# Stores of two chunks with eight tokens per partition, in a scan and mixture-of-adapters kernel

## The chip, the cores and the metric

The kernel runs on one core of a Trainium2 chip. A core has a matrix engine (TensorE, PE in the profile, with its weight loads as PEld), VectorE (DVE), ScalarE (ACT), GpSimd (POOL), and SyncE (SP), which here only issues DMAs. 16 DMA engines move data between HBM and the on-chip memory SBUF; TensorE writes to PSUM, from which VectorE and ScalarE read. The metric is the device time of one execution in microseconds (us), lower is better, given as the median of several runs.

## The reference

Two layers one after the other, on 8 sequences of 6400 tokens with 128 features, all f32:

```python
h = 0                                   # per sequence, 128 features
for t in range(S):
    h = a[:, t] * h + b[:, t]
    x[:, t] = h
# x as (51200, 128)
logits = x @ w_gate                     # 8 experts
topk = the 2 largest of each token;  w = softmax over those two
delta = sum over the 2:  w * ((x @ A[e]) @ B[e])      # A[e]: 128 x 16, B[e]: 16 x 128
out = x + delta
```

The first part is a linear recurrence along the tokens; the second sends each token through two of eight small rank-16 adapters. Inputs a and b are 26.2 MB each and the output is 26.2 MB, so 78.6 MB cross between HBM and the core.

## The kernel before

The 51200 tokens are cut into 100 chunks of 512 tokens (C), and a chunk into four blocks of 128 tokens (J = 4). A chunk is loaded so that partition p holds tokens 4p to 4p + 3 of it, 2 KB in a row; block j then is token 4p + j of every partition p. Most loads take two chunks of a or of b (512 KB), into six buffers each (a_tm, b_tm).

For each chunk (function front):

- A and B: TensorE transposes the four blocks of a and of b against the f32 identity into PSUM (pA, and pB with two buffers), so that features lie on partitions and the 512 tokens of the chunk in order along the row.
- ae: ScalarE copies pA to SBUF (a_st).
- sc: VectorE runs the recurrence over the 512 tokens with one scan instruction (line 442) and writes x in f16 to a ring of 24 chunk buffers (xT). The first value is the last column of the chunk before, so scans form one chain through the whole run. Every 6400 tokens a sequence begins anew; where that falls inside a chunk, its scan is split.

The rest works on units of six blocks (at the end of four), and on groups of four units, 24 blocks or six chunks (at the end of two and one):

- Z (zlogits, line 462): for each block one matmul, with the block of x as the weights that are loaded into TensorE and the adapters A with the gate (128 x 136) as the moving operand. This gives x A for all eight experts and the logits, tokens on partitions. Since tokens of a block are every fourth column of xT, the weight load reads every fourth f16.
- ze: ScalarE copies the result to SBUF (zl).
- gating (g1 to g4 and g6 on VectorE, w1 and w2 on ScalarE, g5, p1, p2, p3 on GpSimd): the largest and second largest logit of each token, the two weights, and a table g of 8 weights per token.
- mu (line 533): GpSimd multiplies zl with g, into zw (f16).
- T (line 543): TensorE transposes the six blocks of zw into pT; te copies them to zwT, on VectorE for three units of a group and on ScalarE for one.
- D (line 558 and 559): for each block, a matmul with the block of x as weights against the f16 identity, which brings x back to tokens on partitions, and on top of it a matmul of zwT with the adapters B. The sum is the output.
- oe (line 569): ScalarE copies it to outt, a ring of 72 blocks.
- st (line 595): SP issues the store of two chunks (of one for the last four).

The order of the work is written out by a planner, a list scheduler inside the kernel file (class Program). Every operation is added with its engine, an assumed duration, what it depends on, and a due time: the start of its period of six chunks (PERIOD) plus an offset from a table (TEMPLATE). For each engine the planner takes the operation that can start first among those whose due time lies within a window (WINDOW) of the earliest one left. LOAD_RATE and STORE_RATE are the DMA rates that it assumes. The result is a fixed order for each engine; semaphore waits are worked out from it. SP issues all loads and stores but the first of b in one queue, so a store that waits holds back the loads behind it.

At the start TensorE runs 34 transposes of the identity (line 359) before and between its first operations.

Of the kernel before, what the change touches and what calls it, by code (L numbers as in the profile page):

```python
# [7 lines left out]
F32 = mybir.dt.float32  # L8
F16 = mybir.dt.float16

PERIOD = 6
# [3 lines left out]
PE_WAIT = 0.08  # L15
SCAN_SELF = 0.13
ISSUE = {"sp": 0.52, "act": 0.45}
LOAD_RATE = 386e3
STORE_RATE = 420e3
DMA_START = 0.3  # L20
DMA_SEEN = 1.15
DMA_DEPTH = 9
FIRST_ISSUE = 0.7
WINDOW = {'pe': 22.339, 'act': 15.032, 'dve': 17.853, 'pool': 31.507, 'sp': 21.093}
START = (-999, "", 0)
FIRST = -9999
TAPER = [2, 2, 1, 1, 1, 1]
# [3 lines left out]
WARM0 = 12  # L31
WARM = 34
LAST = 2
TEMPLATE = {
    "la": [-13.768, -11.488, -10.699],
    "lb": [-11.599, -10.876, -10.408],
    "A": [-8.739, -5.735, -4.61, -4.527, -4.01, -3.388],
    "B": [-0.753, -0.06, 2.522, 2.886, 3.39, 4.151],
    "ae": [6.378, 8.693, 8.757, 9.146, 10.126, 12.233],
    "sc": [11.891, 15.28, 15.373, 17.047, 17.106, 17.222],  # L40
    "Z": [8.614, 8.864, 13.261, 13.471],
    "ze": [17.232, 19.133, 19.801, 20.09],
    "g1": [13.208],
    "g2": [18.458],
    "g3": [3.74],
    "g4": [5.014],
    "g5": [35.276],
    "g6": [5.048],
    "w1": [11.688],
    "w2": [17.689],  # L50
    "p1": [18.712],
    "p2": [4.238],
    "p3": [33.725],
    "mu": [17.377, 18.243, 18.627, 23.065],
    "T": [19.784, 21.14, 23.513, 25.169],
    "te": [11.814, 12.075, 12.746, 13.615],
    "D": [22.711, 24.793, 26.772, 27.207],
    "oe": [23.268, 23.347, 25.158, 27.374],
    "st": [18.431, 19.751, 20.387],
    "ta": [11.3, 11.673, 14.3, 15.8],  # L60
    "md": [10.222, 11.5, 13.0, 14.5],
    "wu": [-0.392],
    "ch": [5.145],
}


# [143 lines left out]
def bass_associative_scan_2x2__then__mixture_of_adapters_kernel(  # L210
# [8 lines left out]
    NB, S, D = a.shape  # L219
# [3 lines left out]
    T = NB * S  # L223
    C = 512
# [11 lines left out]
    b0 = 0  # L236
# [4 lines left out]
    NU = len(units)  # L241

    GMAX = 4
    groups = []
    u0 = 0
    for n in [GMAX] * ((NU - sum(TAPER)) // GMAX) + TAPER:
# [9 lines left out]
    NL = 6  # L256
    HC = 2
    NA = 3
    NX = 24
    NZ = 120  # L260
    NG = 5
    NW = 3
# [10 lines left out]
    with ExitStack() as stack:  # L273
# [19 lines left out]
        a_tm = sbuf("a_tm", [128, HC, J, D], F32, NL)  # L293
        b_tm = sbuf("b_tm", [128, HC, J, D], F32, NL)
        a_st = sbuf("a_st", [128, C], F32, NA)
        xT = sbuf("xT", [128, C], F16, NX)
        zl = sbuf("zl", [128, NZ, W], F32)
        zw = sbuf("zw", [128, U, 128], F16, NW)
        zwT = sbuf("zwT", [128, U * 128], F16, NW)
# [72 lines left out]
        def get(d, k):  # L372
            return [(d[k], True)] if k in d else []

        def xblock(b):
            return xT[b // J % NX].rearrange("d (p j) -> d j p", j=J)[:, b % J, :]

        def te_act(u):
            return u // GMAX < (NU - sum(TAPER)) // GMAX and u % GMAX in TE_ACT
# [31 lines left out]
        def front(c):  # L411
            sl = c // HC % NL
            r0 = rows[c]

            def trans(dst, src):
                def f():
                    dv = dst.rearrange("d (p j) -> d j p", j=J)
                    for j in range(J):
                        last = eng["pe"].transpose(dv[:, j, :], src[:, j, :], ident_f[:, :])  # L419
# [12 lines left out]
            x = xT[c % NX]  # L432
            starts = sorted({0} | {n * S - r0 for n in range(NB) if 0 < n * S - r0 < C})
            segs = list(zip(starts, starts[1:] + [C]))

            def scan():
                for s0, s1 in segs:
                    if (r0 + s0) % S == 0:
                        init = 0.0
                    else:  # L440
                        init = xT[(c - 1) % NX][:, C - 1 : C]
                    last = eng["dve"].tensor_tensor_scan(  # L442
                        out=x[:, s0:s1], data0=a_st[c % NA][:, s0:s1], data1=pB[c % 2][:, s0:s1],
                        initial=init, op0=ALU.mult, op1=ALU.add,
                    )
                return last

            o_sc[c] = P.add("dve", f"sc{c}", 1.276 + 0.16 * (len(segs) - 1),
                            [(o_ae[c], True), (o_B[c], True)] + get(o_sc, c - 1)
                            + get(xlast, c % NX),  # L450
                            scan, fr(c, "sc"))
# [70 lines left out]
        def back(gi, u):  # L522
# [38 lines left out]

            o_D[u] = P.add("pe", f"D{u}", 0.112 * n, [(o_te[u], True)] + get(o_oe, u - 1), delta, ba(gi, u, "D"))
            for k in range(n):
                xlast[(b0 + k) // J % NX] = o_D[u]
            o0 = b0 % NO

            def oe():
# [13 lines left out]
            while True:  # L581
                c = stored[0]
                m = 2 if c < NCH - 4 else 1
                if c >= NCH or (c + m) * J > b0 + n:
                    break
                store(c, m)
                stored[0] += m

        def store(c, m):
            q = c * J % NO  # L590
# [2 lines left out]
            op = P.add(  # L593
                "sp", f"st{c}", m * C * D * 4 / STORE_RATE, [(x, True) for x in src.values()],
                lambda: eng["sp"].dma_start(
                    out[r0 : r0 + m * C, :].rearrange("(h p j) d -> p h j d", p=128, j=J),
                    outt[:, q : q + m * J, :].rearrange("p (h j) d -> p h j d", j=J)),
                (PERIOD * (c // PERIOD), "st", c % PERIOD // 2), sem=dma_sem(f"st{q // (2 * J)}" if m == 2 else f"stx{c % 4}"),
            )
            o_st[c] = op  # L600
            for k in range(m * J):
# [3 lines left out]
        for gi, (u0, n) in enumerate(groups):  # L605
            for u in range(u0, u0 + n):
                b0, m = units[u]
                while nf * J < b0 + m:
                    if nf < 4:
                        load(nf, 1)  # L610
                    elif nf >= NCH - LAST:
# [7 lines left out]
            gating(gi)  # L619
            for u in range(u0, u0 + n):  # L620
                back(gi, u)

        P.schedule()
        waits = P.waits(s_eng, s_dma)
# [64 lines left out]
```

## Time and profile before

| | |
|---|---|
| median of 3 runs | 208.33 us (208.28 to 208.99) |
| profiled execution | 209.08 us |
| its span, first to last instruction | 206.9 us |
| granted TensorE clock, mean | 0.992 |
| busy PE, DVE, ACT, POOL | 94%, 87%, 83%, 64% of the span |
| HBM read and written | 52.56 and 26.21 MB, 381 GB/s over the span |
| pair store, issue to landing (median) | 11.2 us |
| single store, issue to landing (median) | 2.6 us |
| scan of 512 tokens | 1275 ns |

How to read it: the page shows the span in 40 slices, 5.2 us each, with the busy share of each engine in tenths, and the bytes moved by DMA in each slice. A group line names the source line, the engine, the operation, what it writes and reads, its shape and count, then busy time and mean duration, then the idle time of the engine before such instructions and what ended it. Matmuls are pipelined: one is recorded for some 220 to 280 ns, but the next starts 56 to 109 ns after it, so the time that TensorE needs is counted by starts. "Idle before" matters only on an engine that sets the pace.

### The profile page before, as it was taken

To read this page: it belongs to the slowest core of one execution; us is meant where nothing else is said; L and a number is where in the kernel's file an instruction comes from. 1 tells how busy PE (TensorE), PEld (TensorE's weight loads), DVE (VectorE), ACT (ScalarE), POOL (GpSimd) and SP (SyncE) were. 2 spreads that over 40 slices of the span, in tenths; PEclk is the share of its full clock that TensorE was granted. 3 is DMA by queue.
4 is the path that set the end of the run, shared out by engine and by line. 5 is a ranking of instruction groups with operands and counts; after the bars stand their busy time and mean duration, and the time that the engine had idled before them with its cause. 6 is when DMAs were issued, how large, how long until landed. Compare 5 with 4: busy or idle time off the path is not lost.

```text
span 206.9 us, 6064 instructions
## 1 busy us (share of the span) xinstructions
PE 194.1 (94%) x2434; PEld 185.8 (90%) x2434; DVE 179.2 (87%) x266; ACT 172.5 (83%) x295; POOL 132.8 (64%) x156
## 2 busy tenths in 40 slices
PE   6988699999999999999999999999999999998762
PEld 6976589999999999999999999999999999997641
DVE  0379959999999999999999999999998989978871
ACT  2266949979999999999989898989998989898552
POOL 1000194868686776859594949494959494879960
PEclk9999969999999999999999999999999999999999
DMA  6999999999999999999999999999999999999784
GB/s 195 376 388 385 388 387 387 386 395 399 397 397 400 405 394 403 395 402 403 395 407 398 405 395 404 402 400 406 398 405 400 405 401 401 406 406 389 303 333 159
DMA packets 42251, 79.17 MB, mean 383 GB/s; under 512 B 3696, under 2 KB 3824, under 8 KB 42224
## 3 DMA queue, kind: packets, MB, share of 16 engines
q1 hardware_dynamic: 40752, 78.39, 100.0%
q10 hardware_dynamic: 1472, 0.40, 0.8%
q8 instruction: 19, 0.31, 0.6%
q14 instruction: 8, 0.07, 0.1%
HBM read 52.56 MB, written 26.21 MB: 381 GB/s over the span
## 4 chain that ended last, share of the span: by engine, by line
PE 88%; ACT 4%; DVE 3%; POOL 2%; issue 2%; DVEq 0%; POOLq 0%
PE pB L419 21%; PE pA L419 21%; PE pZ L462 12%; PE pO L558 11%; PE pT L543 10%; PE pO L559 10%; PE pO L359 3%; DVE xT L442 2%; POOL zw L533 1%; ACT zl L468 1%; ACT outt L569 1%; ACT a_st L430 1%; DVE zwT L552 1%; ACT L506 1%; POOL g L518 0%
## 5 line engine op out<-in xcount | busy, mean ns | idle before, releaser
L442 DVE TENSOR_TENSOR_SCAN xT<-a_st,xT,pB 128x512 f16<-128x512 f32 x96 | 120.3, 1253 | 9.1 <-PE pB L419 3.5
L533 POOL TENSOR_TENSOR zw<-zl,g 128x768 f16<-128x768 f32 (+1 forms) x66 | 96.3, 1488 | 1.6
L430 ACT COPY a_st<-pA 128x512 f32<-128x512 f32 x100 | 60.5, 605 | 16.2 <-PE pA L419 14.6
L419 PE MATMUL pA<-ident_f,a_tm 128*128 128x128 f32 x400 | 61.7, 277 | 1.7 <-ACT a_st L430 1.5
L569 ACT COPY outt<-pO 128x768 f32<-128x768 f32 (+1 forms) x68 | 55.0, 808 | 9.3 <-PE pO L559 7.7
L419 PE MATMUL pB<-ident_f,b_tm 128*128 128x128 f32 x400 | 61.3, 279 | 1.2 <-DVE xT L442 1.1
L468 ACT COPY zl<-pZ 128x816 f32<-128x816 f32 (+1 forms) x68 | 57.9, 851 | 2.7 <-PE pZ L462 2.4
L558 PE MATMUL pO<-ident_h,xT 128*128 128x128 f16 x400 | 52.2, 220 | 3.6 <-ACT outt L569 1.5
L559 PE MATMUL pO<-cst_h,zwT 128*128 128x128 f16 x400 | 52.0, 219 | 0.0
L558 PEld LDWEIGHTS pO<-ident_h,xT 128*128 128x128 f16 x400 | 44.5, 113 | 5.4 <-ACT outt L569 2.7
L419 PEld LDWEIGHTS pA<-ident_f,a_tm 128*128 128x128 f32 x400 | 45.3, 143 | 3.8 <-issue 2.2
L419 PEld LDWEIGHTS pB<-ident_f,b_tm 128*128 128x128 f32 x400 | 44.3, 143 | 2.7 <-DVE xT L442 1.5
L501 POOL TENSOR_TENSOR dd<-m 128x24 f32<-128x24 f32 (+2 forms) x21 | 7.0, 333 | 51.2 <-DVE m L499 51.2
L559 PEld LDWEIGHTS pO<-cst_h,zwT 128*128 128x128 f16 x400 | 39.3, 98 | 0.0
L462 PE MATMUL pZ<-cst_h,xT 128*128 128x136 f16 x400 | 35.2, 224 | 0.8 <-DVE xT L442 0.4
L543 PE MATMUL pT<-ident_h,zw 128*128 128x128 f16 x400 | 33.5, 219 | 1.0 <-POOL zw L533 0.9
L552 DVE COPY zwT<-pT 128x768 f16<-128x768 f16 (+1 forms) x53 | 28.1, 530 | 5.0 <-PE pT L543 4.8
L462 PEld LDWEIGHTS pZ<-cst_h,xT 128*128 128x128 f16 x400 | 29.7, 114 | 1.9 <-DVE xT L442 0.9
L543 PEld LDWEIGHTS pT<-ident_h,zw 128*128 128x128 f16 x400 | 26.3, 98 | 2.5 <-POOL zw L533 1.8
L514 POOL TENSOR_TENSOR t<-k,w 128x192 f32<-128x192 f32 (+2 forms) x21 | 9.5, 453 | 11.6 <-ACT w L506 11.2
L442 DVE TENSOR_TENSOR_SCAN xT<-a_st,pB 128x512 f16<-128x512 f32 (+1 forms) x8 | 7.5, 939 | 5.6 <-ACT a_st L430 5.5
L549 ACT COPY zwT<-pT 128x768 f16<-128x768 f16 x15 | 12.2, 815 | 0.0
(22 smaller groups left out, 80.9 us busy)
## 6 DMA issues: line engine op xcount, KB each, us to landing
a_tm<-in_a_dram SPq DMA_DIRECT2D x48, 512.0 KB, 11.2
b_tm<-in_b_dram SPq DMA_DIRECT2D x48, 512.0 KB, 11.2
out_dram<-outt SPq DMA_DIRECT2D x48, 512.0 KB, 11.2
a_tm<-in_a_dram SPq DMA_DIRECT2D x4, 256.0 KB, 4.5
out_dram<-outt SPq DMA_DIRECT2D x4, 256.0 KB, 2.6
b_tm<-in_b_dram SPq DMA_DIRECT2D x3, 256.0 KB, 5.5
b_tm<-in_b_dram ACTq DMA_DIRECT2D x1, 256.0 KB, 3.6
cst_f<-in_moe_A_dram ACTq DMA_DIRECT2D x1, 64.0 KB, 4.5
```

The source lines that it names most:

```text
L419: last = eng["pe"].transpose(dv[:, j, :], src[:, j, :], ident_f[:, :])
L430: lambda: eng["act"].copy(a_st[c % NA][:, :], pA[:, :]), fr(c, "ae"))
L442: last = eng["dve"].tensor_tensor_scan(out=x[:, s0:s1], data0=a_st[c % NA][:, s0:s1], data1=pB[c % 2][:, s0:s1], initial=init, op0=ALU.mul ...
L462: last = eng["pe"].matmul(pZ[:, k // (n // 2), o : o + W], xblock(b0 + k), Awg_h)
L468: return eng["act"].copy(zl[:, zb : zb + n, :].rearrange("p (h k) w -> p h (k w)", h=2), pZ[:, :, 0 : n // 2 * W])
L533: lambda: eng["pool"].tensor_tensor(out=wv, in0=zv, in1=gv, op=ALU.mult), ba(gi, u, "mu"))
L543: last = eng["pe"].transpose(pT[:, k * 128 : k * 128 + 128], zw[w][:, k, :], ident_h[:, :])
L549: lambda: eng["act"].copy(zwT[w][:, 0 : n * 128], pT[:, 0 : n * 128]), ba(gi, u, "ta"))
L552: lambda: eng["dve"].tensor_copy(zwT[w][:, 0 : n * 128], pT[:, 0 : n * 128]), ba(gi, u, "te"))
L558: eng["pe"].matmul(dst, xblock(b0 + k), ident_h[:, :], start=True, stop=False)
L559: last = eng["pe"].matmul(dst, zwT[w][:, k * 128 : k * 128 + 128], B_h, start=False, stop=True)
L569: return eng["act"].copy(outt[:, o0 : o0 + n, :].rearrange("p (h k) w -> p h (k w)", h=2), pO[:, :, 0 : n // 2 * 128])
```

## The change

Chunks are joined into pairs (SUP = 2), except the last four, which stay single (SUP_TAIL). A buffer of x now holds a pair, 1024 tokens, and there are 12 of them instead of 24 of one chunk. A block of a pair takes every eighth token: block k is token 8p + k of the pair for every partition p. Loads, transposes and scans stay as they were, chunk by chunk; a scan writes its half of the pair's buffer. Since a block now has tokens of both chunks, Z of a unit depends on the scan of the last chunk of the pair that its last block belongs to (ready). The weight loads of x in Z and D read every eighth f16 of a row. In the output ring a partition holds the eight tokens 8p to 8p + 7 in a row, so a pair store writes 4 KB from each partition to 4 KB of HBM, where it wrote two rows of 2 KB.

The planner's tables (TEMPLATE, WINDOW, LOAD_RATE, STORE_RATE) have other values, so the order of the work changes on every engine. After the last D, TensorE issues 40 transposes of the f32 identity or parts of it (probe): 12 of 64 rows, 4 of 128, 12 of 32, 6 of 128 and 6 of 64. Nothing reads what they write.

```diff
-LOAD_RATE = 386e3
-STORE_RATE = 420e3
+LOAD_RATE = 392e3
+STORE_RATE = 410e3
-WINDOW = {'pe': 22.339, 'act': 15.032, 'dve': 17.853, 'pool': 31.507, 'sp': 21.093}
+WINDOW = {'pe': 39.992, 'act': 58.192, 'dve': 31.37, 'pool': 40.466, 'sp': 30.329}
+SUP = 2
+SUP_TAIL = [1, 1, 1, 1]
 TEMPLATE = {
...
+    supers = []
+    c0 = 0
+    for n in [SUP] * ((NCH - sum(SUP_TAIL)) // SUP) + SUP_TAIL:
+        supers.append((c0, n))
+        c0 += n
+    of_chunk = {c0 + k: i for i, (c0, n) in enumerate(supers) for k in range(n)}
+    ready = {b: supers[of_chunk[b // J]][0] + supers[of_chunk[b // J]][1] - 1 for b in range(NBLK)}
...
-    NX = 24
+    NX = 12
...
-        xT = sbuf("xT", [128, C], F16, NX)
+        xT = sbuf("xT", [128, SUP * C], F16, NX)
...
+        def xcols(c):
+            i = of_chunk[c]
+            o = (c - supers[i][0]) * C
+            return xT[i % NX][:, o : o + C]
+
         def xblock(b):
-            return xT[b // J % NX].rearrange("d (p j) -> d j p", j=J)[:, b % J, :]
+            i = of_chunk[b // J]
+            c0, n = supers[i]
+            return xT[i % NX][:, 0 : n * C].rearrange("d (p j) -> d j p", j=n * J)[:, b - c0 * J, :]
...
         def zlogits(u):
             b0, n = units[u]
-            c1 = (b0 + n - 1) // J
+            c1 = ready[b0 + n - 1]
...
-                    out[r0 : r0 + m * C, :].rearrange("(h p j) d -> p h j d", p=128, j=J),
-                    outt[:, q : q + m * J, :].rearrange("p (h j) d -> p h j d", j=J)),
+                    out[r0 : r0 + m * C, :].rearrange("(p j) d -> p j d", p=128),
+                    outt[:, q : q + m * J, :]),
...
+        def probe(pos):
+            def f():
+                for k in range(12):
+                    h = k % 2
+                    eng["pe"].transpose(
+                        pB[h][:, 0:64], ident_f[64 * h : 64 * h + 64, :], ident_f[64 * h : 64 * h + 64, 64 * h : 64 * h + 64])
+                for k in range(4):
+                    eng["pe"].transpose(pA[:, 0:128], ident_f[:, :], ident_f[:, :])
+                for k in range(12):
+                    h = k % 4
+                    dst = (pB[0], pB[1], pA, pT[:, 0:1024].bitcast(F32))[h]
+                    eng["pe"].transpose(
+                        dst[:, 0:32], ident_f[32 * h : 32 * h + 32, :], ident_f[32 * h : 32 * h + 32, 32 * h : 32 * h + 32])
+                for k in range(6):
+                    eng["pe"].transpose(pA[:, 0:128], ident_f[:, :], ident_f[:, :])
+                for k in range(6):
+                    last = eng["pe"].transpose(pB[0][:, 0:64], ident_f[0:64, :], ident_f[0:64, 0:64])
+                return last
+            return f
+
+        P.add("pe", "mb", 3.0, [(o_D[uN], True), (o_sc[NCH - 1], True), (o_te[uN], True), (o_ae[NCH - 1], True)],
+              probe(0), (9999, "", 0))
```

More of the change, by code (lines that the diff above doesn't have):

```diff
@@ L33 @@
 LAST = 2
+SUP = 2
+SUP_TAIL = [1, 1, 1, 1]
 TEMPLATE = {
[L35 to L63, printed above, removed]
+    "la": [-10.95, -9.437, -8.191],
+    "lb": [-10.023, -9.436, -7.903],
+    "A": [-11.026, -8.648, -7.41, -6.832, -6.44, -5.405],
+    "B": [-14.825, -14.817, -14.221, -14.015, -13.001, -10.71],
+    "ae": [-7.284, -6.693, -6.603, -5.642, -5.031, -4.184],
+    "sc": [13.472, 14.407, 15.428, 17.663, 19.382, 19.457],
+    "Z": [18.437, 19.004, 20.556, 22.524],
+    "ze": [51.529, 54.024, 54.601, 57.134],
+    "g1": [25.622],
+    "g2": [7.661],
+    "g3": [5.296],
+    "g4": [1.145],
+    "g5": [43.458],
+    "g6": [25.384],
+    "w1": [16.708],
+    "w2": [54.97],
+    "p1": [39.689],
+    "p2": [7.051],
+    "p3": [12.642],
+    "mu": [18.896, 19.36, 19.457, 24.196],
+    "T": [28.309, 28.632, 31.127, 33.058],
+    "te": [24.866, 24.891, 26.352, 29.891],
+    "D": [31.247, 32.555, 33.577, 36.679],
+    "oe": [46.479, 48.831, 48.877, 50.195],
+    "st": [21.173, 26.136, 27.083],
+    "ta": [11.3, 12.233, 14.3, 15.8],
+    "md": [9.107, 11.5, 13.0, 14.5],
+    "wu": [19.523],
+    "ch": [-28.476],
+    "mb": [0.0],
 }
@@ L243, in bass_associative_scan_2x2__then__mixture_of_adapters_kernel @@
     GMAX = 4
+    supers = []
[3 more added lines that the diff above has]
+        c0 += n
+    assert c0 == NCH
+    of_chunk = {c0 + k: i for i, (c0, n) in enumerate(supers) for k in range(n)}
+    ready = {b: supers[of_chunk[b // J]][0] + supers[of_chunk[b // J]][1] - 1 for b in range(NBLK)}
     groups = []
@@ L430, in front @@
                             lambda: eng["act"].copy(a_st[c % NA][:, :], pA[:, :]), fr(c, "ae"))
-            x = xT[c % NX]
+            x = xcols(c)
             starts = sorted({0} | {n * S - r0 for n in range(NB) if 0 < n * S - r0 < C})
@@ L440, in scan @@
                     else:
-                        init = xT[(c - 1) % NX][:, C - 1 : C]
+                        init = xcols(c - 1)[:, C - 1 : C]
                     last = eng["dve"].tensor_tensor_scan(
@@ L449, in front @@
                             [(o_ae[c], True), (o_B[c], True)] + get(o_sc, c - 1)
-                            + get(xlast, c % NX),
+                            + get(xlast, of_chunk[c] % NX),
                             scan, fr(c, "sc"))
@@ L563, in back @@
             for k in range(n):
-                xlast[(b0 + k) // J % NX] = o_D[u]
+                xlast[of_chunk[(b0 + k) // J] % NX] = o_D[u]
             o0 = b0 % NO
@@ L580, in back @@
                 olast[(b0 + k) % NO] = o_oe[u]
[L581 to L587, printed above, removed]
+            while stored[0] < len(supers) and sum(supers[stored[0]]) * J <= b0 + n:
+                store(*supers[stored[0]])
+                stored[0] += 1
         def store(c, m):
@@ L595, in store @@
                 lambda: eng["sp"].dma_start(
-                    out[r0 : r0 + m * C, :].rearrange("(h p j) d -> p h j d", p=128, j=J),
-                    outt[:, q : q + m * J, :].rearrange("p (h j) d -> p h j d", j=J)),
-                (PERIOD * (c // PERIOD), "st", c % PERIOD // 2), sem=dma_sem(f"st{q // (2 * J)}" if m == 2 else f"stx{c % 4}"),
+                    out[r0 : r0 + m * C, :].rearrange("(p j) d -> p j d", p=128),
+                    outt[:, q : q + m * J, :]),
+                (PERIOD * (c // PERIOD), "st", c % PERIOD // 2), sem=dma_sem(f"st{q // (SUP * J)}" if m == SUP else f"stx{c % 4}"),
             )
@@ L607, in bass_associative_scan_2x2__then__mixture_of_adapters_kernel @@
                 b0, m = units[u]
-                while nf * J < b0 + m:
+                while nf <= ready[b0 + m - 1]:
                     if nf < 4:
@@ L621, in bass_associative_scan_2x2__then__mixture_of_adapters_kernel @@
                 back(gi, u)
+        def probe(pos):
[17 more added lines that the diff above has]
+            return f
+        uN = NU - 1
+        P.add("pe", "mb", 3.0, [(o_D[uN], True), (o_sc[NCH - 1], True), (o_te[uN], True), (o_ae[NCH - 1], True)],
+              probe(0), (9999, "", 0))
         P.schedule()
```

## The prediction

> **What bounds the kernel now.** I read the page's slices first, then the three matmul weight-load groups, then the busy time of each engine by stage, then VectorE's and TensorE's timelines. The slices say that three resources are full at once:
>
> ```profile
> span 206.9 us, 6064 instructions
> ...
> PE   6988699999999999999999999999999999998762
> ...
> DVE  0379959999999999999999999999998989978871
> ...
> DMA  6999999999999999999999999999999999999784
> GB/s 195 376 388 385 388 387 387 386 395 399 397 397 400 405 394 403 395 402 403 395 407 398 405 395 404 402 400 406 398 405 400 405 401 401 406 406 389 303 333 159
> ```
>
> The DMA engines are busy from about 2 us to about 187 us: 387 GB/s while only loads run, some 401 GB/s once stores (a third of the bytes) are mixed in. The stages:
>
> ```profile
> 96.00:132.00 36.00, 35.99 (x481) 35.79 (x480) 34.53 (x49) 33.86 (x57) 25.65 (x26) 1.00 1.05 401
> ...
> 156.00:186.00 30.00, 29.61 (x388) 28.46 (x386) 27.05 (x45) 27.23 (x47) 22.03 (x23) 1.00 1.05 403
> 186.00:206.90 20.90, 13.40 (x178) 10.67 (x176) 13.39 (x35) 11.66 (x27) 13.47 (x28) 1.00 0.79 298
> ```
>
> (columns: stretch, length, busy PE, PEld, DVE, ACT, POOL, clock, DMA share, GB/s). A busy PE overlaps its own instructions, so I use the spacing of matmul starts: 109 ns for an f32 transpose, 56 for an f16 matmul, 59 for the 136-wide one. Six chunks hold 48, 72 and 24 of these: 10.7 us. VectorE takes the same time for six chunks, without a gap:
>
> ```profile
> 100.16 1.27 DVE L442 TENSOR_TENSOR_SCAN xT<-a_st,xT,pB 128x512 f16<-128x512 f32 x1
> 101.35 0.53 DVE L552 COPY zwT<-pT 128x768 f16<-128x768 f16 x1
> 101.80 1.27 DVE L442 TENSOR_TENSOR_SCAN xT<-a_st,xT,pB 128x512 f16<-128x512 f32 x1
> 103.00 0.56 DVE L552 COPY zwT<-pT 128x768 f16<-128x768 f16 x1
> 103.47 2.69 DVE L442 TENSOR_TENSOR_SCAN xT<-a_st,xT,pB 128x512 f16<-128x512 f32 x2
> 106.08 0.53 DVE L552 COPY zwT<-pT 128x768 f16<-128x768 f16 x1
> ...
> 109.12 0.33 DVE L489 TENSOR_REDUCE m<-zl 128x24 f32<-128x192 f32 x1
> 109.49 0.36 DVE L491 TENSOR_TENSOR k<-zl,m 128x192 f32<-128x192 f32 x1
> ...
> 110.94 1.27 DVE L442 TENSOR_TENSOR_SCAN xT<-a_st,xT,pB 128x512 f16<-128x512 f32 x1
> ```
>
> From 100.16 to 110.94 is one period of six chunks, 10.78 us, or 1.80 us a chunk. DMA needs 786 KB a chunk: 1.96 us at 401 GB/s. So the compute engines lead at 1.80 from chunk 48 to 72 (91.3 to 134.4 us, living on loads made ahead), and DMA leads after that: the A transposes of chunks 72 and 99 start at 134.4 and 186.5, 1.93 us a chunk. From 186 us a dependent tail of small groups ends the run, with every engine under 65% busy.
>
> **The change, part by part.**
>
> *Store packets.* 48 pair stores go from 256 packets of 2 KB to 128 of 4 KB. The trace's packet records have medians of 27 ns for 512 B and 84 for 2,048; the least of the 8,192 B instruction fetches took 309. The line through these gives 159 to 160 ns for 4,096 B, against 2 x 84 = 168: 8.5 ns saved per pair of packets, 128 x 8.5 / 16 engines = 0.07 us a store, 3.3 us for all 48. Bounds: nothing (packets overlap: the DMA share is 1.05), or 309/2 = 154.5 ns, 5.2 us in all. I take 3.3, as the 2 KB and 8 KB rows lie on both sides.
>
> The Trainium skill ("DMA: Bandwidth & Descriptors", Why small descriptors are slow) states a fixed overhead of about 3 cycles a packet. At the 850 MHz of that page (Where 436 GB/s comes from) this is an estimated 3.5 ns, 1.3 us in all; the intercept of the trace's rows is 8 ns. By the page the forecast would be about 1.3 us higher.
>
> *Order of the DMAs.* In SP's built order 34 pair stores stood before the last load and 14 behind it; now it is 32 and 16. Two stores fewer are 2 x 0.524 MB at 401 GB/s, 2.6 us. With 32 x 0.07 = 2.2 us, DMA lets the last load land 4.8 us earlier. (A store waits for both its chunks in either kernel; SP's queue holds behind it only loads, as before.)
>
> *May compute follow?* At 1.80 us instead of 1.93, chunks 72 to 99 take 3.5 us less. By the built order TensorE has, when it starts chunk 99's A, done 342 blocks of T and 330 of D instead of 354 and 348: 12 x 0.056 + 18 x 0.112 = 2.7 us less. Together 6.2; DMA's 4.8 is the smaller, so the front ends 4.8 us earlier.
>
> *VectorE's order.* Gating steps now alternate with scans (in letters, S scan, t zwT copy, digits gating: S t S S 1 t S S 2 3 S 4 t 6, before S t S t S S t S S 1 2 3 4 6). Pitches from the timeline: scan then scan 1.41, scan then something else 1.20, copy then scan 0.45, a gating step before its dependent 0.37 to 0.39, before something else 0.27. The new period sums to 10.4 instead of 10.78 us. What is late next is TensorE at 10.7: worth at most 0.1 us a period, no more.
>
> *Weight loads of x.* A block of x was read every fourth f16 (8 bytes apart), now every eighth (16 bytes). No row has a 16-byte step. The nearest:
>
> ```profile
> L558 PEld LDWEIGHTS pO<-ident_h,xT 128*128 128x128 f16 x400 | 44.5, 113 | 5.4 <-ACT outt L569 2.7
> L419 PEld LDWEIGHTS pB<-ident_f,b_tm 128*128 128x128 f32 x400 | 44.3, 143 | 2.7 <-DVE xT L442 1.5
> L543 PEld LDWEIGHTS pT<-ident_h,zw 128*128 128x128 f16 x400 | 26.3, 98 | 2.5 <-POOL zw L533 1.8
> ```
>
> Packed f16 98 ns, 8-byte step 113, f32 143. What counts is how long the load alone holds back its matmul. A matmul after idle shows it:
>
> ```profile
> 201.65 0.25 PE L558 MATMUL pO<-ident_h,xT 128*128 128x128 f16 x1 [0.52 <-DVE zwT L552]
> 201.73 0.22 PE L559 MATMUL pO<-cst_h,zwT 128*128 128x128 f16 x1
> ```
>
> It is recorded from its load's start to its end: 250 ns against 220 in a run, so 30 ns of load; by the same subtraction in the trace's records packed f16 has 15 and f32 331 - 273 = 58. In a run a load starts 2 ns after the matmul ahead started, so it is hidden while it is below the slot, 56 ns (59 for Z). Below: 30 ns again, cost 0. Above: the 109 ns spacing of the f32 transposes, if loads rather than matmuls set it: 400 x 53 + 400 x 50 = 41 us. I take 58 (f32's row, and about twice 30, as 30 is twice 15): 2 to 4 ns over the slot in D, none to 1 in Z, 24 x 4 ns = 0.1 us a period. TensorE goes from 10.7 to 10.8, which VectorE took before: 0 in the sum. Its cover is that 0.1 us; beyond, each ns on all 800 loads is 0.8 us on the path.
>
> The Trainium skill ("SBUF — State Buffer", Specifications) wants at least two hits in a 16-byte line for full bandwidth: that speaks against a 16-byte step, which has one. Its Door 1 section lists a stride of 8 bf16 as free in the same breath. No row here decides it. By the first reading the sum loses what lies over the slot, by the second nothing.
>
> *The ring of x* holds 12 pairs instead of 24 chunks and frees them by pair. D of the first block starts at 32.4 us, the scan that reuses its place is that of chunk 24, whose A starts at 47.4: 15 us cover a delay of one chunk, cost 0; without the cover, one chunk, 1.8 us.
>
> *Start.* Pairs delay Z: before the first T, TensorE now issues 60 B and 48 Z blocks instead of 56 and 42, 4 x 0.109 + 6 x 0.059 = 0.8 us. Ends: 0 (it waits there anyway, 18.65 busy of 22 us from 8 to 30), and one scan pitch, 1.4. I take 0.4.
>
> *Tail.* What was deferred returns: after the last B the order has 61 T, 70 D, 16 Z, 4 A blocks instead of 46, 52, 12, 0: 3.5 us of TensorE; VectorE gets three more copies and four small gating steps after the last scan, about 2.6 us. Ends: 0 (engines are under 65% busy) and 3.5. I take 3.0, for the tail is a dependent chain.
>
> *The 40 transposes of the identity* follow the last D on TensorE; nothing waits for them but the end. In the old trace the last D started at 203.58 and the span ended at 206.9: 3.3 us of cover (copy, store, landing). At 109 ns each they take 4.4 us; with the 30 narrow ones at the f32 load's 58 ns, 2.8. With 0.28 latency and 0.15 for the end barrier they stick out by 0 to 1.5 us. I take 0.2, as narrow ones move at most 64 columns.
>
> **Sum** on the span: -4.8 + 0.4 + 3.0 + 0.2 = -1.2, 205.7 us. The profiled execution took 209.08 us, 2.18 around its span; the median of the runs shown is 208.33, 0.75 below it. On the median: 207.1 us.
>
> **Rivals.**
> 1. *The weight loads overrun their slot.* For: 98, 113, 143 grow with the spread. Against: 58 ns still nearly fits. At 10 ns over in all 800: 8 us, less the 0.8 us of cover (0.1 x 8 periods): 214.3. Place: above all the gap-free stretch, 48 to 156 us. It decides against the forecast from 3 ns over on all loads (2.4 less 0.8 is more than 1.2 gained).
> 2. *The tail returns everything,* or the packets save nothing while only the order moves: the front gains 2.6 to 4.8, the tail gives 3.5 back: 208.0 to 209.
> 3. *Everything works:* loads hidden (10.7, 0.1 us a period, 0.8 less), tail half absorbed (1.5 less): 204.8.
> 4. *The identities show:* 1.5 us at the end instead of 0.2: 208.4.
>
> **How the numbers follow.** Forecast 0.40 (own range 206.0 to 208.3), rival 1 0.22, rival 2 0.17, rival 3 0.13, rival 4 0.08. A measurement of this kernel tells about 0.5%, 1.04 us, from no change. Faster: 0.27 of the forecast, all of 3, 0.04 of the others, 0.44. Same: 0.13 of the forecast, 0.10 of 2 and 4: 0.23. Slower: rival 1 and the rest, 0.33. The range 204.5 to 213 leaves out about 0.12 above (loads over by 9 ns or more) and 0.04 below.
>
> **What the profile after would show.** Packets of 4 KB at about 160 ns; above 405 GB/s in the mixed stage; weight loads of x near 140 ns, D's matmuls 58 to 60 ns apart; VectorE with gaps in mid-run; chunk 99's A near 182 us; TensorE ending within 0.3 us of the last store. The prediction is wrong if D's spacing passes 65 ns or the tail grows by over 4 us.

## The result, and the profile after

The changed kernel takes 213.43 us (median of 6 runs, 212.92 to 214.62); the kernel before, on the same chip, 208.59 us (6 runs). The ratio is 1.0238, with a 95% interval of 1.0206 to 1.0270: 2.4% slower. The forecast was 207.1 us, and 213.43 lies just above the upper end of its range, 213.0. The profiled execution took 214.0 us, with a span of 212.1. Two executions of kernels told below, of 234.25 us at a granted clock of 0.855 and of 499.64 us, stand far apart from the others of the same kernel and are left out of the times and ratios given here.

The slices of the page after (40 slices of 5.3 us):

```profile
span 212.1 us, 6151 instructions
...
PE   6999799999999999999999999999999999988669
...
DVE  0599789989999999999989898989899998986640
...
DMA  7999999999999999999999999999999999986472
GB/s 198 378 387 385 386 388 385 387 397 406 393 406 399 400 401 403 394 402 403 403 406 401 407 397 404 401 405 404 402 404 404 405 403 410 413 334 264 188 275 102
```

VectorE now has gaps in mid-run (8 where it had 9), the sign that was expected if it stopped being a bound. DMA moves what it moved before. TensorE shows no gap from 27 to 185 us, and in the last slice it rises again to 9. The stages, with the columns of the table before the change:

```profile
96.00:132.00 36.00, 36.00 (x472) 35.82 (x471) 33.31 (x47) 33.73 (x57) 26.14 (x27) 1.00 1.04 402
156.00:186.00 30.00, 29.77 (x388) 29.24 (x386) 28.12 (x42) 26.82 (x46) 23.35 (x24) 1.00 1.04 405
186.00:212.10 26.10, 20.18 (x244) 16.01 (x242) 13.23 (x42) 13.72 (x31) 14.06 (x30) 0.89 0.59 231
```

Between 96 and 132 us TensorE is as busy as before, within 0.01 us, but it does 472 matmuls in that time instead of 481: 2% less work in full time. The groups of the weight loads say where to look:

```profile
L577 PEld LDWEIGHTS pO<-ident_h,xT 128*128 128x128 f16 x400 | 49.8, 143 | 6.4 <-ACT outt L588 5.5
L578 PEld LDWEIGHTS pO<-cst_h,zwT 128*128 128x128 f16 x400 | 42.5, 106 | 0.0
...
L481 PEld LDWEIGHTS pZ<-cst_h,xT 128*128 128x128 f16 x400 | 32.3, 144 | 0.6 <-ACT zl L487 0.3
L562 PEld LDWEIGHTS pT<-ident_h,zw 128*128 128x128 f16 x400 | 26.3, 98 | 2.7 <-POOL zw L552 0.8
```

The loads of x (577 in D, 481 in Z) take 143 and 144 ns instead of 113 and 114, and even the packed load that follows each of them in D (578) went from 98 to 106, while the one in T (562) stayed at 98. The load's mean says little by itself, since it overlaps the matmul ahead. TensorE's timeline, where the first column is the start, says what it costs:

```profile
120.48 0.23 PE L577 MATMUL pO<-ident_h,xT 128*128 128x128 f16 x1
120.55 0.22 PE L578 MATMUL pO<-cst_h,zwT 128*128 128x128 f16 x1
120.60 0.23 PE L577 MATMUL pO<-ident_h,xT 128*128 128x128 f16 x1
120.67 0.22 PE L578 MATMUL pO<-cst_h,zwT 128*128 128x128 f16 x1
120.72 0.23 PE L577 MATMUL pO<-ident_h,xT 128*128 128x128 f16 x1
```

One D block takes 120 ns instead of 112. Over all records the median spacing within a D block went from 56 to 64 ns, the one from a block to the next stayed at 56, and that of Z went from 59 to 62. The 16 blocks of the last four chunks, which stay single, keep the 8-byte step; 384 x 8 + 384 x 3 ns is 4.2 us more for TensorE in the whole run. By the starts of the A transposes of chunks 36 and 60 a period of six chunks takes 10.99 us instead of 10.78.

How that moves the run, by the start of the A transposes of some chunks and of the last copy to outt (us, profiled executions; the last two columns belong to experiments that are told below):

| | before | after | after, 8-byte step | before, 16-byte step |
|---|---|---|---|---|
| A of chunk 24 | 47.4 | 46.1 | 46.1 | 47.6 |
| A of chunk 48 | 91.3 | 90.3 | 89.2 | 92.4 |
| A of chunk 72 | 134.4 | 134.4 | 132.4 | 136.6 |
| A of chunk 99 | 186.5 | 184.8 | 181.8 | 189.7 |
| last copy to outt | 203.8 | 207.2 | 203.6 | 207.2 |
| end of the span | 206.9 | 212.1 | 207.8 | 210.3 |

The new order is ahead by 1.3 us at chunk 24 and loses that lead up to chunk 72. That first row is not firm: in two more profiles with the order of before up to there (the identities, and the second buffer, in the kernel before, both told below) chunk 24 starts at 46.8 and 45.5 us, and in the profile of before the granted clock is at half from 26.7 to 30.1 us. From chunk 24 to 99 the profiles agree better: 139.1 us before, with and without the identities, 138.7 after, 135.7 with the 8-byte step. At chunk 99 the changed kernel is 1.7 us ahead, where 4.8 were forecast, and the tail from there to the last copy takes 22.4 us instead of 17.3. Then 4.9 us pass to the end, where 3.1 did before.

### The profile page after: what moved, and what is told of

It is laid out like the page before. It is cut to its first block, busy times and chain, and to the rows that moved or that the text cites. A ratio compares the mean times of both kernels' runs of the same rounds, so it can differ in the third digit from the quotient of the medians.

```text
span 212.1 us, 6151 instructions
## 1 busy us (share of the span) xinstructions
PE 201.3 (95%) x2474; PEld 192.7 (91%) x2474; DVE 178.4 (84%) x266; ACT 175.3 (83%) x295; POOL 130.7 (62%) x156
## 4 chain that ended last, share of the span: by engine, by line
PE 79%; ACT 7%; DMA 6%; SPq 4%; DVE 3%; issue 1%; DVEq 0%
PE pB L438 18%; PE pA L438 17%; PE pO L577 12%; PE pO L578 10%; PE pZ L481 10%; PE pT L562 9%; DMA b_tm<-in_b_dram 6%; ACT outt L588 4%; SPq L421 4%; DVE xT L461 2%; ACT a_st L449 1%; ACT zl L487 1%; PE pA L652 1%; ACT L525 1%; PE pA L645 0%
## 5 line engine op out<-in xcount | busy, mean ns | idle before, releaser
L449 ACT COPY a_st<-pA 128x512 f32<-128x512 f32 x100 | 58.9, 589 | 16.2 <-PE pA L438 14.8
L438 PE MATMUL pA<-ident_f,a_tm 128*128 128x128 f32 x400 | 60.5, 274 | 1.3 <-ACT a_st L449 1.1
L577 PE MATMUL pO<-ident_h,xT 128*128 128x128 f16 x400 | 55.8, 229 | 4.5 <-ACT outt L588 4.2
L487 ACT COPY zl<-pZ 128x816 f32<-128x816 f32 (+1 forms) x68 | 56.6, 833 | 3.6 <-PE pZ L481 1.9
L577 PEld LDWEIGHTS pO<-ident_h,xT 128*128 128x128 f16 x400 | 49.8, 143 | 6.4 <-ACT outt L588 5.5
L578 PE MATMUL pO<-cst_h,zwT 128*128 128x128 f16 x400 | 55.1, 220 | 0.0
L438 PEld LDWEIGHTS pA<-ident_f,a_tm 128*128 128x128 f32 x400 | 45.9, 141 | 2.6 <-ACT a_st L449 1.8
L578 PEld LDWEIGHTS pO<-cst_h,zwT 128*128 128x128 f16 x400 | 42.5, 106 | 0.0
L520 POOL TENSOR_TENSOR dd<-m 128x24 f32<-128x24 f32 (+2 forms) x21 | 5.1, 245 | 55.2 <-DVE m L518 55.0
L481 PEld LDWEIGHTS pZ<-cst_h,xT 128*128 128x128 f16 x400 | 32.3, 144 | 0.6 <-ACT zl L487 0.3
L537 POOL TENSOR_TENSOR g<-g,t 128x192 f32<-128x192 f32 (+2 forms) x21 | 10.7, 509 | 1.3
```

The source lines that it names most:

```text
L487: return eng["act"].copy(zl[:, zb : zb + n, :].rearrange("p (h k) w -> p h (k w)", h=2), pZ[:, :, 0 : n // 2 * W])
L577: eng["pe"].matmul(dst, xblock(b0 + k), ident_h[:, :], start=True, stop=False)
L578: last = eng["pe"].matmul(dst, zwT[w][:, k * 128 : k * 128 + 128], B_h, start=False, stop=True)
```

## The experiments

Theory 1 is rival 1 of the prediction: the weight loads overrun their slot. Theory 2 is that the identities hold up the end. Against both stands the order: that the new tables or the dependence on pairs cost the time, whatever the loads take. Each ratio is to the kernel before as measured beside that run; differences between kernels are taken from the medians unless the ratios are named.

### One suspect at a time, in the changed kernel

**The identities left out.**

```diff
-        P.add("pe", "mb", 3.0, [(o_D[uN], True), (o_sc[NCH - 1], True), (o_te[uN], True), (o_ae[NCH - 1], True)],
-              probe(0), (9999, "", 0))
```

> The changed kernel without the 40 transposes of the identity at the end. In the changed kernel's profile the last D starts at 206.88 us, the last store has landed by 210.5 and TensorE ends at 211.85. If the transposes set the end (my theory for about a quarter of the loss): 1.0 to 1.4 us less than the changed kernel, 212.0 to 212.4. If they are covered by the last store: no difference beyond 0.3 us, 213.1 or more.

Measured: 212.04 us, ratio to before 1.0159 [1.0141, 1.0177]. That is 1.4 us less than the changed kernel by the medians, 1.6 by the ratios, with an interval of 0.9 to 2.4. The DMA view says how 40 instructions whose results nobody reads can hold up a store. From 203 to 212 us in the changed kernel:

```profile
q1 hardware_dynamic: 720, 1.57, 46.1%
q8 instruction: 1, 0.02, 0.6%
```

and in the kernel without them:

```profile
q1 hardware_dynamic: 720, 1.57, 45.7%
```

The program is longer, so one more piece of it, 16 KB, is fetched: from 208.1 to 209.0 us in the changed kernel, while the 16 DMA engines write the last store. One engine's share of the store lands at 210.5, the other shares by 209.8. Without the identities the last fetch begins at 193.7, and all shares land together at 209.7. All five kernels shown here that have the identities have such a fetch in the last 5 us of their span and one late share, and a longer fetch goes with a later share: fetches of 0.93, 1.21, 1.26, 1.48 and 1.48 us, shares 0.7, 1.0, 1.1, 1.1 and 1.2 us late. Of the twelve others none has a fetch in the last 10 us, and in eleven the shares land together; in the twelfth (the kernel before with a second buffer, told below) one share is 1.3 us late with no fetch near it. So a share can be late for another reason too. That the fetch delays it here is read from the traces; no run keeps the identities and takes the fetch away. In this one profile something comes on top: the granted clock falls to half from 206.5 us on, and the identities themselves end last.

```profile
206.88 0.31 PE L578 MATMUL pO<-cst_h,zwT 128*128 128x128 f16 x1
207.13 0.90 PE L642 MATMUL pB<-ident_f 64*128 64x64 f32 x12
207.96 1.12 PE L645 MATMUL pA<-ident_f 128*128 128x128 f32 x4
...
209.47 1.54 PE L652 MATMUL pA<-ident_f 128*128 128x128 f32 x6
210.94 0.90 PE L654 MATMUL pB<-ident_f 64*128 64x64 f32 x6
```

They take 4.7 us here; in the next experiment, at full clock, 2.8, as the prediction had it. Of the changed kernel's six runs two had less than full clock (0.987 and 0.992, 214.00 and 214.62 us), and the other four took 212.92 to 213.69, so a part of the 1.4 us, some 0.3 by the medians, may be the clock.

**The step of the weight loads back to 8 bytes**, all else as changed:

```diff
-  return xT[i % NX][:, 0 : n * C].rearrange("d (p j) -> d j p", j=n * J)[:, b - c0 * J, :]
+  return xT[i % NX][:, 0 : n * C].rearrange("d (h p j) -> d h j p", h=n, j=J)[:, (b - c0 * J) // J, b % J, :]
```

> The changed kernel with one edit: a block of x is read at a step of 4 f16 (8 bytes) again, with every order, store and buffer as in the changed kernel. Blocks then hold other tokens, so rows of the output of a pair stand in other places than the reference's; no work is left out. Theory A (weight loads at a 16-byte step overrun their slot): the load is 113 instead of 143 ns, D's matmuls 56 instead of 64 and 56 alternately, 24 blocks take 10.7 instead of 11.0 us, and the time falls by 3 to 4.5 us, to 209.0 to 210.4. Theory B (the new order with its longer tail loses the time, loads do not matter): less than 1 us, 212.4 or more.

Measured: 209.62 us, ratio 1.0041 [1.0026, 1.0056]: 3.8 us less than the changed kernel (by the ratios 4.1), with the identities still in. Its groups, and D in its timeline:

```profile
L577 PEld LDWEIGHTS pO<-ident_h,xT 128*128 128x128 f16 x400 | 44.5, 113 | 5.1 <-ACT outt L588 3.9
L578 PEld LDWEIGHTS pO<-cst_h,zwT 128*128 128x128 f16 x400 | 39.4, 98 | 0.0
```

```profile
121.89 0.22 PE L577 MATMUL pO<-ident_h,xT 128*128 128x128 f16 x1
121.94 0.22 PE L578 MATMUL pO<-cst_h,zwT 128*128 128x128 f16 x1
122.00 0.22 PE L577 MATMUL pO<-ident_h,xT 128*128 128x128 f16 x1
```

The spacing is 56 again, in Z 59, and the packed load is back at 98. The third column of the table above is this kernel: with 1.80 us a chunk from 48 to 72 instead of 1.84 it keeps its lead and is at chunk 99 at 181.8 us, as the forecast had it (near 182).

**The stores' rows back to 2 KB**, all else as changed:

```diff
-                    out[r0 : r0 + m * C, :].rearrange("(p j) d -> p j d", p=128),
-                    outt[:, q : q + m * J, :]),
+                    out[r0 : r0 + m * C, :].rearrange("(h p j) d -> p h j d", p=128, j=J),
+                    outt[:, q : q + m * J, :].rearrange("p (h j) d -> p h j d", j=J)),
```

> The changed kernel with pair stores of two 2 KB rows again, everything else unchanged; rows of a pair land in other places than the reference's, no work is left out. If the 4 KB packets gain what the forecast said for the part before the last load and this reaches the end: 2 to 3 us more, 215.4 to 216.4. If TensorE at 11.0 us per six chunks leaves DMA a cover: within 0.7 us of the changed kernel, 212.7 to 214.1.

Measured: 213.55 us, ratio 1.0223 [1.0206, 1.0240]. No difference from the changed kernel can be told. A 4 KB packet takes 159 ns in the records, two of 2 KB take 168, as predicted, but the time does not follow. That fits TensorE setting the pace, as the second expectation has it.

**The planner's tables of before** (TEMPLATE, WINDOW and the two rates) in the changed kernel:

> The changed kernel with the planner's tables of the kernel before (TEMPLATE, WINDOW and both rates); pairs, 4 KB rows and the identities at the end stay. Theory A (loads and identities make the loss): within 1.2 us of the changed kernel, 212.2 to 214.6. Theory B (the new order makes the loss): 3 us less or more than that, 210.4 or below.

Measured: 220.04 us (three runs), ratio 1.0553 [1.0522, 1.0585], 6.6 us more than the changed kernel, which neither expectation had. The new tables do not cost the time; pairs need them.

### The same step, and the same identities, in the kernel before

The last two suspects can also be put into the kernel before by themselves. Two chunks share one buffer of x there, one on the even and one on the odd f16, so that a block is read with a 16-byte step while order, dependences and stores stay. (A buffer of twice the length for each chunk, with the ring cut to 19 chunks, did not fit into SBUF: 768 bytes a partition were needed and 96 left.)

```diff
-        xT = sbuf("xT", [128, C], F16, NX)
+        xT = sbuf("xT", [128, C, 2], F16, NX // 2)
...
-            return xT[b // J % NX].rearrange("d (p j) -> d j p", j=J)[:, b % J, :]
+            c = b // J
+            return xT[c // 2 % (NX // 2)][:, :, c % 2].rearrange("d (p j) -> d j p", j=J)[:, b % J, :]
```

> The kernel before with one edit: two chunks of x share a buffer of twice the length, one on its even and one on its odd f16, so that a block is read at a 16-byte step; order, stores, blocks and the size of the ring are as before. Theory A: weight loads of x go from 113 to 143 ns, D's matmuls from 56 to 64 and 56 alternately, Z from 59 to 62; 24 blocks take about 11.0 instead of 10.8 us; 2.5 to 4.5 us slower than before, 211.3 to 213.3. Rival (it is not the step but the pairs' layout or the order that lengthens D): within 0.6 us of before. A slower scan (now 1275 ns) would show that writing 4 bytes apart costs VectorE something by itself.

Measured: 212.35 us, ratio 1.0192 [1.0160, 1.0223], 3.8 us more than the kernel before (by the ratio 4.0).

```profile
L559 PEld LDWEIGHTS pO<-ident_h,xT 128*128 128x128 f16 x400 | 50.4, 144 | 5.9 <-ACT outt L570 3.3
...
L463 PEld LDWEIGHTS pZ<-cst_h,xT 128*128 128x128 f16 x400 | 33.0, 146 | 1.5 <-DVE xT L443 0.8
```

The scan, which now writes every second f16, still takes 1275 ns; the spacing in D is 64 and in Z 63. So the step alone costs what taking it away gives back: 3.8 us either way by the medians.

The 40 transposes of the identity added to the kernel before:

> The kernel before with the 40 transposes of the identity behind its last D, all else as before. Theory C (they cost through the end, in part because they bring one more 16 KB instruction fetch, which holds one DMA engine's share of the last store): 0.6 to 1.4 us slower, with a fetch after 200 us and one share of the last store 0.6 to 1.0 us behind the other fifteen. Rival (the loss came with the new order alone): within 0.3 us of before.

Measured: 209.34 us (12 runs, 208.09 to 210.13), ratio 1.0020 [0.9999, 1.0041]: 0 to 0.9 us, less than in the changed kernel and between the two expectations. The fetch is there (204.0 us, 1.48 us long), one share of the last store lands at 207.0 and the others by 205.9, while the identities end at 206.0, ahead of the end. That their cost depends on where the fetch falls against the last store is likely, but no run shows it.

### What is left of the change without both

**8-byte step and no identities** (the first two edits together):

> The changed kernel with both suspects taken out: a block of x read at an 8-byte step (rows of the output of a pair stand in other places than the reference's, no work is left out) and no transposes of the identity at the end. What is left of the change is pairs, the new order and 4 KB rows. If the two losses add (3.8 and 1.4 us as each measured alone): 208.0 to 208.5 us, 0.1 to 0.4% below the kernel before. If new order and 4 KB rows gain the 1.2 us or more that the forecast had for them: 207.6 or below. If the losses overlap: 208.9 or more.

Measured: 208.48 us (12 runs), ratio 0.9986 [0.9971, 1.0001]. Pairs, 4 KB rows and the new order together gain 0.3 us, with an interval that just touches nothing.

**The same with 2 KB rows**, which gives the output of before:

> As the kernel with an 8-byte step and no identities, but pair stores write two 2 KB rows: this is the layout and output of the kernel before, with pairs and the new order only. Theory (4 KB packets pay once TensorE is back at 10.7 us per six chunks and DMA limits chunks 84 to 99): 0.7 to 2.2 us slower than with 4 KB rows. Rival (packets are hidden here too): within 0.4 us of it.

Measured: 209.00 us (12 runs), ratio 1.0011 [0.9998, 1.0024]. The long rows are worth 0.5 us (0.1 to 0.9), again between the two expectations; for all 48 stores the prediction had 3.3. The profiles do not show where: A of chunk 99 starts at 182.2 us with 4 KB rows and at 182.1 with 2 KB.

**x packed, so that a block is 128 f16 in a row**, with 4 KB rows and no identities:

```diff
-  return xT[i % NX][:, 0 : n * C].rearrange("d (p j) -> d j p", j=n * J)[:, b - c0 * J, :]
+  return xT[i % NX][:, (b - c0 * J) * 128 : (b - c0 * J) * 128 + 128]
```

> As the changed kernel without identities, but a block of x is 128 f16 in a row (the output's rows stand in other places, no work is left out). Theory A (a load costs only what it is longer than its matmul's slot of 56 ns): load 98 ns, D's spacing 56 as at the 8-byte step, and the time within 0.6 us of the kernel with an 8-byte step and no identities, 207.9 to 209.1. Rival (each ns of load counts): a further 1.5 us or more less, 207.0 or below.

Measured: 208.29 us (10 runs), ratio 0.9985 [0.9968, 1.0003]. Its loads take 98 ns instead of 113, and the time is that of the 8-byte step. A load that fits its slot costs nothing, however long it is; only what lies over the slot counts.

### The order and the tail

**Orders exchanged.** The kernel before with the new tables:

> The kernel before with the changed kernel's planner tables, all else as before. If the new order is better in itself (VectorE at 10.4 us per six chunks, an earlier front): 207.0 to 208.2. If it only fits pairs: 210 or above.

Measured: 215.48 us, ratio 1.0348 [1.0277, 1.0419]. And the old tables with pairs, 8-byte step and no identities:

> The kernel with pairs and 4 KB rows, 8-byte step (rows of the output of a pair in other places) and no identities, but with the planner's tables of the kernel before. If the old order does not fit pairs whatever the loads cost: 213 to 217, some 5 to 8 us above the same kernel with the new tables (208.5). If old order and slow loads only hurt together: below 210.5.

Measured: 216.64 us, ratio 1.0393 [1.0367, 1.0420]. Either set of tables loses 3.5 to 4% with the other layout. They are a part of their layout, and no measurement splits the change into "order" and "pairs".

**Where the lead goes.** Without step and identities A of chunk 99 starts at 182.2 us, 4.3 ahead of before, and yet the last copy to outt starts at the same 203.84. A stretch of that kernel's chain of waits (start, length, what):

```profile
197.36 0.05 issue
197.41 0.25 PE pO L577
...
198.21 0.07 PE pO L578
198.28 0.02 issue
198.31 0.81 ACT outt L588
199.11 0.05 issue
199.16 0.25 PE pO L577
```

D of a unit writes to pO, ScalarE copies pO out, and the next D may begin only then: 1.75 us for a unit whose matmuls need 0.67. To tell whether this is what holds the tail, D of units 64 and 66 of 68 was given the buffer pZ, which no Z needs by then, in the kernel with 8-byte step, 2 KB rows and no identities (209.00 us):

```diff
+        alt = set(range(NU - 4, NU, 2))
...
+            pD = pZ if u in alt else pO
...
-                    dst = pO[:, k // (n // 2), o : o + 128]
+                    dst = pD[:, k // (n // 2), o : o + 128]
...
-            o_D[u] = P.add("pe", f"D{u}", 0.112 * n, [(o_te[u], True)] + get(o_oe, u - 1), delta, ba(gi, u, "D"))
+            o_D[u] = P.add("pe", f"D{u}", 0.112 * n, [(o_te[u], True)] + get(o_oe, u - 2 if u >= min(alt) else u - 1), delta, ba(gi, u, "D"))
...
+        for u in alt:
+            o_D[u].deps.append((o_ze[NU - 1], True))
```

The copy reads the same pD. ("The run before it" in the next text is the one with three units on pZ, told below.)

> As the run before it, but only units 66 and 64 write to pZ, and nothing is held back: the second buffer alone. Theory A: up to two waits of 0.7 us fall away, 207.6 to 208.6. Theory B, and a mixture in which the gating of the last units stands ready to take over as soon as D is quicker: 208.7 to 209.2.

Measured: 208.12 us (12 runs), ratio 0.9978 [0.9967, 0.9990]: 0.7 us less than the same kernel with one buffer (by the ratios, 0.3 to 1.1). The chain from 186 us on, by line, with one buffer:

```profile
by line: ACT outt L588 15.0%; POOL zw L552 12.8%; PE pO L577 11.2%; issue 8.6%; PE pO L578 7.8%; PE pT L562 6.5%; DVE zw L556 5.4%; DVE zwT L571 3.5%; POOL g L537 3.1%; POOL t L533 1.3%; POOL g L535 1.3%; DVE k L522 0.9%; POOLq L645 0.1%
```

and with two:

```profile
by line: POOL zw L553 21.6%; issue 8.8%; DVE zwT L572 6.0%; PE pT L563 5.4%; POOL g L537 5.1%; ACT outt L591 5.0%; POOL g L535 4.5%; PE pO L580 3.3%; POOL t L533 3.1%; PE pO L581 1.9%; DVE L L512 1.9%; ACT w L525 1.8%; PE pZ L580 1.7%; POOL
```

The copy falls from 15.0 to 5.0% and GpSimd's multiplication and gating take its place. The time is theory A's; the chain shows in addition what theory B named. The turns on pO do hold the tail, and a second chain, the gating of the last units, stands some 0.7 us behind them.

Then the order of the last 14 units was changed as well, by a table of delays (HOLD, 0.3 to 2.5 us) that the planner adds when it chooses the next operation of an engine; the table came from a search for the earliest end by the planner's own durations. First with three units on pZ:

```diff
+HOLD = {"D54": 0.3, "D55": 1.0,
...
-                    t = max(free[e], ready[op.i])
+                    t = max(free[e], ready[op.i]) + HOLD.get(op.name, 0.0)
...
+        alt = set(range(NU - 6, NU, 2))
```

> Pairs, 8-byte step, 2 KB rows and no identities, which took 209.0 us. Now three of the last six units (66, 64 and 62) have D write to pZ, which no Z needs any more, so that D of a unit need not wait for the copy of the one before; and the planner holds back some operations of the last 14 units, so that the order of the tail makes use of it. All is computed. Theory A (the tail is held by D and its copy taking turns on pO, 1.75 us a unit): three of the last five turns lose the 0.6 to 0.8 us of waiting, 1.5 to 2.4 us in all, so 206.6 to 207.5. Theory B (the tail is held by the gating of the last units or by the stores): within 0.5 us of 209.0.

Measured: 208.96 us, ratio 1.0019 [1.0002, 1.0036]: a miss for theory A as put there. The same kind of table with one buffer:

> Pairs, 8-byte step, 2 KB rows, no identities, one buffer for D, and an order of the last 14 units from the same search as in the first run of this call. Theory A: without the second buffer order alone gains nothing, 208.7 to 209.2. Theory B in the form that only the order of the gating in the tail was bad: most of the gain of the first run, below 208.3.

Measured: 210.18 us, ratio 1.0085 [1.0062, 1.0108], by the ratios 1.5 us slower than without the table, which neither theory had. By the planner's durations these two kernels should have gained 2.4 us (buffers and table) and 0.1 us (table alone) on the one without either. The table alone does harm; what the buffers are worth beside a table is open, since the two kernels have different tables. Of the planner's picture of the tail, differences of 2 us can't be trusted.

The kernel before, with two units on pZ and such a table:

> The kernel before with D of units 66 and 64 written to pZ and an order of the last 14 units that makes use of it. Its chain in the tail goes through gating, the multiplication on GpSimd and the copy of zwT, and D waits for its own copy less often. Theory A: it gains less than the pairs do, 0.3 to 1.2 us, 207.3 to 208.3. Theory B: nothing, 208.2 to 208.8.

Measured: 208.16 us (11 runs), ratio 0.9977 [0.9962, 0.9992]: 0.5 us faster than before, in theory A's range and just below theory B's. Buffer and table came together here, and no run separates them. In its profile the last copy to outt starts at 201.9 us, 1.9 ahead of before, but the end comes only 0.6 earlier, because one share of the last store lands 1.3 us after the others. The fastest kernel that computes the reference is thus one of these two, 0.2% below the kernel before, and neither has the 16-byte step.

## Why the prediction was wrong, by its own steps

**The step that failed: weight loads of x, "0 in the sum".** The load by itself was sized about rightly. Behind idle, a D matmul at the 16-byte step is now recorded with 276 to 282 ns, against 219 to 220 without a wait, so 56 to 63 ns of load where 58 were taken. What failed is the next sentence, "2 to 4 ns over the slot in D, none to 1 in Z". The spacing of 64 in D and 62 in Z shows 8 and 3 ns over. In a run the D matmul with the strided load is recorded with 228 ns instead of 219, so the wait falls on that matmul itself, and the record of the packed load behind it grows by as much, from 98 to 106. By the prediction's own sum (the load, plus the 2 ns after which it starts, less the slot of 56) 56 to 63 ns are 2 to 9 over: an estimate that is good to a few ns could not decide about a slot that is 2 ns away, yet it went into the sum as 0. Its series of "15", 30 and 58 was not firm either: behind idle the records of before mostly give 10 to 11 ns for a packed f16 load, 27 to 30 for the 8-byte step, and for f32 54 to 57 in some and 26 to 30 in others. That the f32 loads hide was no support, because their matmul needs 109 ns.

The cover was smaller than taken as well. From chunk 36 to 60 a period took 10.78 us before, 10.73 with pairs and the 8-byte step, and 10.99 in the changed kernel: 0.05 us of cover instead of 0.1, against an overrun of 24 x 11 ns, 0.26. Rival 1 had the mechanism. Its 0.8 us for each ns on all loads makes 4.2 us of a mean of 5.5 ns on 768 loads; measured were 3.8 both by removing the step and by adding it (4.1 and 4.0 by the ratios). The sign of being wrong "D's spacing passes 65 ns" was set too high, 64 was enough; the other, a tail that grows by over 4 us, came true with 5.1.

The Trainium skill ("SBUF — State Buffer", Specifications) asks for two hits in a 16-byte line, and that reading fits the slow case of these runs: 143 ns with one f16 in a line, 113 with two. Full bandwidth at two hits would make 113 as short as the 98 of a packed load, which it is not; the slot hides that difference. The reading of its Door 1 section, that a stride of eight bf16 is free, does not hold for these f16 weight loads.

**The identities, 0.2 us taken with an upper end of 1.5: measured 1.4 in the changed kernel (0.9 to 2.4), 0.4 in the old one.** Their length was right, 2.8 us at full clock. The step looked only at TensorE against the last store, where the cover was enough. The price came in another way: by the traces through the fetch of their code beside the last store, and in some runs through the clock.

**Store packets, 3.3 us (2.2 before the last load): 0 in the changed kernel, 0.5 without its losses.** The recorded duration was right to 1 ns (159 against 159 to 160), but the records of packets overlap: among the start times the differences of 80 ns (2 KB) and 155 ns (4 KB) stand out. By these a long row saves 5 ns and not 8.5, 0.04 us a store, 1.9 us in all. Nor did the lead hang on DMA in most of the run: from 48 to 186 us it moved 399 to 405 GB/s, not above 405.

**Order of the DMAs and compute, -4.8 us: -4.3 with the 8-byte step and no identities.** "Chunk 99's A near 182" came out at 182.2, but with some luck. 2.2 of the 4.8 were the packets, and with 2 KB rows A of chunk 99 starts at 182.1 all the same. And a part of the 4.3 lies ahead of chunk 24, where executions of one order differ by 1.9 us; from chunk 24 to 99 the gain is 3.4 us (2.9 with 2 KB rows). In the changed kernel the loads left 1.7 of the 4.3.

**VectorE's order and the ring of x: right.** VectorE got gaps, TensorE led at 10.73 us a period with the 8-byte step, and nothing shows a wait for a place in the ring.

**Start, +0.4 us: not confirmed.** A of chunk 24 came 1.3 us earlier in the profile, not later, but profiles of the old order have it at 45.5 to 47.4 and those of the new one at 45.9 to 46.6, so a difference of 0.4 can't be told. It has no weight of its own, since the front's 4.3 us includes it.

**Tail, +3.0 us with an upper end of 3.5: +4.3 by itself, +5.1 with the slow loads.** It was priced by TensorE's work, 0.112 us for each deferred D block. But in the tail D takes turns with its copy on one buffer, 1.75 us a unit of six blocks, which is 0.29 a block. Three units deferred cost 5.2 us by that row instead of 2.0, if nothing runs beside them; that two units with a second buffer gained only 0.7 us fits a gating chain that covers a part of this anyway. Rival 2, that the tail returns everything, was right on the change without its two losses (208.48 in its 208.0 to 209).

Together, by the two profiles: -1.3 up to chunk 24, -0.5 from there to chunk 99, +5.1 in the tail to the last copy and +1.8 from there to the end make 5.1 us; the spans differ by 5.2. By the runs: -0.3 for pairs, order and rows, +1.4 to 1.6 for the identities and +3.8 to 4.1 for the loads make 4.9 to 5.4; the medians differ by 4.8.

## What to carry to other kernels

Where the engine that sets the pace runs without a gap, measure how far its hidden work is from the edge of its cover before trusting a cover of 1%: a weight load that fits its slot is free at 98 and at 113 ns, and one that overran its slot cost 8 ns each time in D and 3 in Z, 3.8 us in all. Price work that is deferred into a tail by the dependent chain there (here 1.75 us a unit, for D and its copy on one buffer), not by the busy time of one engine. And code at the end of a program is not free because nobody waits for its result: it has to be fetched, and here the fetch fell beside the last store, one share of which came late.

## What the runs showed of the hardware that was not expected

- The record of a packed weight load behind one with a 16-byte step is longer, 106 instead of 98 ns, in the order of before as in the new one, and back at 98 when the step goes.
- Records of DMA packets overlap: a 2 KB packet is recorded with 84 ns and a 4 KB one with 159, but starts 80 and 155 ns apart are by far the most frequent.
- A 16 KB instruction fetch takes 0.9 to 1.5 us. Fetches come about every 10 us throughout the run; in the five profiles where one falls beside the last store, one engine's share of it landed 0.7 to 1.2 us after the others. A share was 1.3 us late once without a fetch.
- f32 transposes of 64 rows start closer than those of 128 rows (109 ns apart): at full clock two on different halves of the rows start 3 to 4 ns apart and the next pair some 60 ns later, so 12 take 0.5 us; six on the same rows start 63 ns apart.
- The granted clock fell to half in the tail of one profile, 5.6 us before the end. In the other four profiles with identities it stayed at full up to the end. In the order of before it is at half for 3.4 us near the start in two profiles (from 26.7 us before, from 26.4 with the 16-byte step) and not in two others.
